# Attention, expert MLPs and a dense MLP on one core: units in turned order, two preparations a unit, last weights' halves moved

## The chip, the core and the metric

One core of a Trainium2 chip runs the whole program. The metric is the device time in microseconds (us) of one execution; of before there are three timed runs. The engines are named as in the profile: PE (TensorE; PEld is its weight load), DVE (VectorE), ACT (ScalarE), POOL (GpSimd), SP (SyncE, which here only issues DMAs).

## What is computed

Three stages, each fed by the one before; everything is float32 outside.

```python
# 1. attention: q, k, v are [4, 8, 576, 64]; heads 0-3 "plain", heads 4-7 "dilated"
scores = q @ k.T / 8
mask_plain = (rel >= 0) & (rel < 32)                       # rel = query - key
mask_dil = (rel >= 0) & (rel < 128) & (rel % 4 == 0)
attn = softmax(where(mask, scores, -1e9)) ; x = attn @ v   # -> [2304, 512] tokens
# 2. mixture of experts, 8 experts, top 1
xn, en = x / |x|, expert_emb / |expert_emb|
logits = xn @ en.T / 0.1 ; e = argmax ; gate = softmax(logits)[e]
y = gate * (relu(x @ w1[e]) @ w2[e])                       # w1 [8,512,1024], w2 [8,1024,512]
# 3. dense MLP with a per-column leak
h = y @ w_in ; g = max(h, 0) + alpha * min(h, 0) ; out = g @ w_out   # w_in [512,2048]
```

## The kernel before

**Attention** is cut into 44 units (n = 0 to 43, eleven for each of 4 batches). A unit is a block of four (in places two) score tiles of one kind, plain or dilated. It passes through the engines as a pipeline over units: in the body of unit n stand `stage_qk(n)` (mask and scores on PE, row maximum `nm` on DVE, `exp` on ACT), `stage_t(n-1)` (the exponentials are transposed on PE, L437, and brought to SBUF as `pts`), `stage_av(n-2)` (times V on PE into `o`, L458; then DVE takes the row sums, `rs`, their reciprocal and the product `xs`, L463 to L476) and, some units later, `stage_x` (`xs` transposed into `psx`, L513, and copied to `xp`/`xd`) and the router's logits. The PSUM tile `o` has one buffer, so the next AV starts only when DVE has read `o` into `xs`. Between these stand the **preparations**: the next batch's q and k are transposed, four per head pair, the plain ones in 64-column tiles (L362), the dilated ones in 128-column tiles (L365). A table `PLAN` says how many preparations each unit takes: three in most units of the first batch, then two, then one at a batch's end. The products on 64-column tiles (plain preparations and AV) are called narrow here, those on 128 columns (scores, transposes) wide. Each engine executes its instructions in the order in which the code emits them, and an instruction that waits holds all that stands behind it on its engine.

**Routing.** When a group of tokens is through, POOL scatters their numbers into the table `tab_d` (`to_table`, L552, one indirect DMA per 128 tokens), then reads indices back (`x_index`, `ix`), gathers the first slot's tokens (`x_gather`, `xg`) and builds one-hot rows (`hot`, L571 and L573), from which PE makes the ranks (`hot_rows`, `lgf`, L582). These steps hang on the units of the last batch by the list `last`; POOL also splits two of the first weight pieces (L723, L727).

**Expert MLPs.** Nine slots s = 0 to 8 of fixed widths (`WIDTHS`: 192, 256, 408, 360, 328, 312, 296, 272, 256 tokens) run in a row; each has eight steps f. In a step PE makes `hps` (layer 1, `l1`, L810), ACT and DVE split the result into a high and a low part (`hh` L814, `hl` L815), and PE makes `yps` (layer 2, `l2`, L1030) two steps later. Products are in three terms of split operands. A stream of weights is loaded ahead by SP (`w_load`, at most AHEAD = 4 items ahead, five staging tiles `stg`) and split by ACT (`whi`, L725) and DVE or POOL (`wlo`, L727, one instruction of 128x1024). Into the same stream are put the halves of the dense MLP's weights (`z_load`, `z_split`): 32 halves; the split of one is six DVE instructions (L1084 to L1091, tiles `za`, `zb`) and a copy on ACT. Before, a slot takes one half (s = 1), two at f = 0 and 2 (s = 2 to 7), or five at f = 0, 2, 3, 5, 7 (s = 8): 18 halves; the other 14 are split in the first chunk of the dense MLP. `feed(8*s + f)` emits what is due at a step. At f = 1 `y_store` writes the slot before to `y_d`; at f = 0 of slot 8 `y_load(0)` brings the dense MLP's first chunk back, and `y_split(0, f-4)` at f = 4 to 7, behind `feed`, splits it (L1106 on ACT, L1107 on DVE). `overflow` (slot 1) fills the little tile `widths` on POOL (L982) and subtracts it on DVE (L983).

**Dense MLP.** Five chunks of up to 512 tokens, sixteen steps each: `mps` (m1, L1116), the leak on ACT and DVE, `ops` (m2, L1142).

## Time and profile before

| what | us |
|---|---|
| timed runs: median (lowest to highest of 3) | 889.96 (883.88 to 895.82) |
| the profiled execution, its own time | 888.99 |
| span of its trace | 887.2 |
| PE busy in it | 836.1 (94%) |
| PE busy by stage: attention 0 to 187.4 of the span | 167.2 |
| expert MLPs, 187.4 to 467.2 | 263.6 |
| dense MLP, 467.2 to 887.2 | 405.3 |

PE is busy nearly throughout; its clock is granted at full speed (1.0 in the rows, 2.4 GHz) or at half (0.5, 1.2 GHz), and busy time in a stretch at half counts twice. So the time is to be read in two things: where PE stands still, and where it runs at half clock. DVE (52%), ACT (42%) and POOL (23%) have room on the average, but each is in order.

### The profile page before, as it was taken

How to read it: one execution, taken by the hardware profiler on the slowest of the kernel's cores; microseconds unless marked ns; L12 is line 12 of the kernel's file. 1: busy time of each engine (PE TensorE's matmuls, PEld its weight loads, DVE VectorE, ACT ScalarE, POOL GpSimd, SP SyncE). 2: the span in 40 equal slices, each digit the busy share in tenths (PEclk: the TensorE clock that was granted, in tenths of full speed). 3: DMA queues.
4: the chain of work that ended last, by engine and by line, in shares of the span. 5: the costliest groups of instructions: out<-in, count | busy, mean ns of one | idle time of the engine just before them, and what ended most of it. 6: DMA issues, size and time to landing. Idle time of an engine off the chain costs nothing.

```text
span 887.2 us, 15233 instructions
## 1 busy us (share of the span) xinstructions
PE 836.1 (94%) x5887; PEld 731.7 (82%) x5887; DVE 459.3 (52%) x959; ACT 375.7 (42%) x823; POOL 200.1 (23%) x211
## 2 busy tenths in 40 slices
PE   7999999599899999989888999999999999999994
PEld 5888887489899999989877888788888888888893
DVE  3556665356566576665678888622332233223330
ACT  3546665253545545534533443533333333333431
POOL 7100012743364457554410000000010001000100
PEclk8859999689999999989898999999999999999998
DMA  9974933746676998978973560100010001000000
GB/s 179 168 161 88 184 73 63 112 112 139 207 188 144 269 163 179 281 185 134 281 222 95 72 170 1 59 37 1 1 60 36 1 1 42 30 1 1 25 24 26
DMA packets 102093, 93.39 MB, mean 105 GB/s; under 512 B 38770, under 2 KB 83076, under 8 KB 102016
## 3 DMA queue, kind: packets, MB, share of 16 engines
q1 hardware_dynamic: 97472, 81.82, 42.2%
q0 software_dynamic: 4544, 10.54, 3.5%
q8 instruction: 48, 0.79, 0.4%
q14 instruction: 29, 0.24, 0.1%
HBM read 77.08 MB, written 15.27 MB: 104 GB/s over the span
## 4 chain that ended last, share of the span: by engine, by line
PE 70%; DMA 10%; DVE 9%; ACT 5%; issue 3%; POOL 2%; SPq 1%; POOLq 0%; ACTq 0%; DVEq 0%
PE mps L1116 21%; PE ops L1142 21%; PE hps L810 8%; PE yps L1030 7%; DMA stg<-in_moe_w_out_dram 3%; DMA stg<-in_moe_w_in_dram 3%; PE s L419 2%; PE o L458 2%; DMA kld<-in_k_dram 2%; DMA stg<-in_moe_w_dram 2%; ACT pe L426 1%; PE pt L437 1%; PE s L405 1%; PE psq L362 1%; PE psx L513 1%
## 5 line engine op out<-in xcount | busy, mean ns | idle before, releaser
L1128 DVE SCALAR_TENSOR_TENSOR g<-z,nalpha,g 128x512 f32<-128x512 f32 (+1 forms) x80 | 55.6, 695 | 169.7 <-ACT g L1127 169.6
L1116 PE MATMUL mps<-yh,zhi 128*128 128x512 f32 (+1 forms) x320 | 119.1, 372 | 1.8 <-ACT yh L1106 1.8
L1116 PE MATMUL mps<-yl,zhi 128*128 128x512 f32 (+1 forms) x320 | 118.9, 372 | 1.1 <-DVE yl L1107 1.1
L1116 PE MATMUL mps<-yh,zlo 128*128 128x512 f32 (+1 forms) x320 | 118.9, 372 | 0.0
L1154 POOL DMA_INDIRECT out_dram<-osb,cid x18 | 18.4, 1020 | 406.1 <-ACT osb L1153 371.4
L1126 ACT ACTIVATE z<-mps 128x512 f32<-128x512 f32 (+1 forms) x80 | 44.3, 554 | 150.1 <-PE mps L1116 150.1
L1142 PE MATMUL ops<-zhi,gl 128*128 128x512 f32 x256 | 100.9, 394 | 0.2 <-DVE gl L1130 0.2
L1142 PE MATMUL ops<-zhi,gh 128*128 128x512 f32 x256 | 100.8, 394 | 0.0
L1142 PE MATMUL ops<-zlo,gh 128*128 128x512 f32 x256 | 100.4, 392 | 0.0
L727 POOL TENSOR_TENSOR wlo<-stg,whi 128x1024 fp32r<-128x1024 f32 x30 | 75.4, 2513 | 95.0 <-ACT whi L725 94.7
L1030 PE MATMUL yps<-hh,whi 128*128 128x256 f32 (+7 forms) x288 | 91.2, 317 | 3.9 <-ACT hh L814 2.8
L1030 PE MATMUL yps<-hl,whi 128*128 128x256 f32 (+7 forms) x288 | 89.1, 309 | 4.0 <-DVE hl L815 3.9
L1030 PE MATMUL yps<-hh,wlo 128*128 128x256 f32 (+7 forms) x288 | 88.6, 308 | 0.0
L810 PE MATMUL hps<-xl,whi 128*128 128x256 f32 (+7 forms) x288 | 88.1, 308 | 0.3 <-DVE xl L776 0.3
L810 PE MATMUL hps<-xh,whi 128*128 128x256 f32 (+7 forms) x288 | 88.2, 308 | 0.0
L810 PE MATMUL hps<-xh,wlo 128*128 128x256 f32 (+7 forms) x288 | 88.1, 308 | 0.0
L426 ACT ACTIVATE pe<-s,nm 96x80 f32<-96x80 f32 (+1 forms) x168 | 42.0, 328 | 77.2 <-DVE nm L421 56.8
L1116 PEld LDWEIGHTS mps<-yh,zhi 128*128 128x128 f32 x320 | 60.6, 189 | 13.6 <-ACT yh L1106 2.3
L1116 PEld LDWEIGHTS mps<-yl,zhi 128*128 128x128 f32 x320 | 60.5, 189 | 13.7 <-DVE yl L1107 2.3
L725 ACT CAST whi<-stg 128x1024 fp32r<-128x1024 f32 x62 | 64.7, 1044 | 15.4 <-DMA stg<-in_moe_w_dram 14.9
L1116 PEld LDWEIGHTS mps<-yh,zlo 128*128 128x128 f32 x320 | 60.5, 189 | 10.8
L1129 ACT CAST gh<-g 128x512 fp32r<-128x512 f32 x64 | 39.7, 621 | 65.0 <-DVE g L1128 65.0
(228 smaller groups left out, 1696.0 us busy)
## 6 DMA issues: line engine op xcount, KB each, us to landing
stg<-in_moe_w_dram SPq DMA_DIRECT2D x64, 512.0 KB, 9.8
stg<-in_moe_w_in_dram SPq DMA_DIRECT2D x16, 512.0 KB, 9.0
stg<-in_moe_w_out_dram SPq DMA_DIRECT2D x16, 512.0 KB, 6.7
yl<-y_d SPq DMA_DIRECT2D x4, 1024.0 KB, 5.9
kld<-in_k_dram SPq DMA_DIRECT2D x8, 384.0 KB, 7.0
qld<-in_q_dram SPq DMA_DIRECT2D x8, 384.0 KB, 7.1
x_d<-xs SPq DMA_DIRECT2D x32, 96.0 KB, 3.5
vdl<-in_v_dram SPq DMA_DIRECT2D x16, 160.0 KB, 4.2
```

Source lines behind the costliest of these rows:

```text
L419: nc.tensor.matmul(s[0:nq, i, c0:nk], lhsT=lhsT, rhs=rhs, start=False, stop=(i == m - 1))
L426: nc.scalar.activation(out=pe[0:nq, i, :], in_=s[0:nq, i, :], func=AF.Exp, bias=nm[0:nq, i:i + 1])
L725: nc.scalar.copy(hi, s)
L727: eng.tensor_tensor(out=lo, in0=s, in1=hi.bitcast(F32), op=ALU.subtract)
L810: nc.tensor.matmul(ps, lhsT=parts[j][0][:, kk, :], rhs=parts[j][1][:, kk, 0:wd], start=((kk, j) == steps[0]), stop=((kk, j) == steps[-1]))
L1030: nc.tensor.matmul(ypt[s_, d], lhsT=a[:, 128 * d:128 * (d + 1)], rhs=x, start=(f == 0 and j == 0), stop=(f == NF - 1 and j == 2))
L1116: nc.tensor.matmul(ps, lhsT=a[:, kk, :], rhs=x, start=(kk == 0 and j == 0), stop=(kk == KD - 1 and j == 2))
L1126: nc.scalar.activation(out=z, in_=ps, func=AF.Relu, scale=-1.0)
L1128: vec.scalar_tensor_tensor(out=g, in0=z, scalar=nalpha[:, f:f + 1], in1=g, op0=ALU.mult, op1=ALU.add)
L1129: nc.scalar.copy(gh, g)
L1142: nc.tensor.matmul(opt[c, t], lhsT=a[:, 128 * t:128 * (t + 1)], rhs=x, start=(f == 0 and j == 0), stop=(f == NF2 - 1 and j == 2))
L1154: nc.gpsimd.indirect_dma_start(out=out[:, :], out_offset=bass.IndirectOffsetOnAxis(ap=cid[:, 4 * c + t, 0:1], axis=0), in_=o, in_offset=None)
```

## The change

1. `PLAN` becomes `PREPS = 2`: two preparations in every unit.
2. In odd units from n = 3 on the narrow work (plain preparations, AV) is emitted ahead of the wide work (scores, transposes, dilated preparations); in even units the order stays.
3. The first batch's q and k of the dilated heads are loaded ahead of its plain v.
4. In the last batch `to_table` is no longer called after every unit but once, behind two of the three one-hot builds; `hot_rows` of groups 1 and 2 and of group 0 move by a unit or more, the third into slot 0's hooks.
5. `widths` is filled in the setup.
6. POOL's `wlo` is cut in four instructions of 256 columns (for s > 0); DVE's is not.
7. `z_split` works in place, in the staging tile, with one temporary tile in place of two; the staging counter starts at 1.
8. The weights' halves per slot become 1, 3, 3, 2, 2, 1, 1, 4 for s = 1 to 8, at the steps in `ZAT`: 17 in place of 18, so 15 are left for the dense MLP.
9. `y_split(0, .)` comes at f = 3 to 6 of slot 8, ahead of `feed`; `y_load(0)` and slot 0's `y_store` are issued on ACT's queue in place of SP's.

```diff
-    PLAN = ((2, 3, 3, 3, 3, 3, 3, 3, 3, 3, 3), (2, 2, 2, 2, 2, 2, 2, 1, 1, 1, 1))
+    PREPS = 2
...
+    load_qk(0, 0, 1)
     load_vpl(0)
-    load_qk(0, 0, 1)
...
+        for i in range(NS):
+            nc.gpsimd.memset(widths[:, i:i + 1], float(WIDTHS[i]))
...
-    ns_ = [0]
+    ns_ = [1]
...
-        eng.tensor_tensor(out=lo, in0=s, in1=hi.bitcast(F32), op=ALU.subtract)
+        n = 256 if eng is nc.gpsimd and i else 1024
+        for c in range(0, 1024, n):
+            eng.tensor_tensor(out=lo[:, c:c + n], in0=s[:, c:c + n], in1=hi[:, c:c + n].bitcast(F32), op=ALU.subtract)
...
-    for i, f in ((0, regs_a), (0, lambda: x_index(0)), (1, open_early), (1, flush), (1, lambda: x_gather(0)), (1, to_table),
-                 (2, hg(0)), (2, wl(0)), (3, hg(1)), (3, wl(1)), (4, hg(2)), (4, wl(2)), (5, wl(3)), (5, hr(0)), (5, sp(0)),
-                 (6, wl(4)), (6, sp(1)), (7, hr(1)), (8, hr(2)), (9, lambda: x_turn(0, 0)), (10, lambda: x_turn(0, 1))):
+    for i, f in ((0, regs_a), (0, lambda: x_index(0)), (1, open_early), (1, flush), (1, lambda: x_gather(0)), (1, hg(0)),
+                 (2, hg(1)), (2, to_table), (2, wl(0)), (3, hg(2)), (3, wl(1)), (4, wl(2)), (5, wl(3)), (5, sp(0)),
+                 (6, wl(4)), (6, sp(1)), (6, hr(0)), (8, hr(1)), (9, lambda: x_turn(0, 0)), (10, lambda: x_turn(0, 1))):
...
+            def wide():
+                stage_qk(n, u)
...
+            def narrow():
+                some(plains[1])
+                some(plains[0], 1)
+                if n >= 2:
+                    stage_av(n - 2)
+                some(plains[0])
...
+            for f in (narrow, wide) if n % 2 and n > 2 else (wide, narrow):
+                f()
...
-            to_table()
+            if b < 3:
+                to_table()
...
-            nc.sync.dma_start(
+            (nc.sync if s_ else nc.scalar).dma_start(
...
-        a = tmp_p.tile([128, 512], I32, tag="t", name="za")
...
+        vec.tensor_scalar(out=b, in0=whi, scalar1=3, scalar2=0x3FFFFFF8, op0=ALU.logical_shift_left, op1=ALU.bitwise_and)
+        vec.scalar_tensor_tensor(out=whi, in0=whi, scalar=-0x40000000, in1=b, op0=ALU.bitwise_and, op1=ALU.bitwise_or)
+        vec.tensor_scalar(out=b, in0=whi, scalar1=-0x800000, scalar2=None, op0=ALU.bitwise_and)
...
+    ZAT = ((), (0,), (0, 2, 4), (0, 2, 4), (0, 3), (0, 3), (2,), (2,), (2, 3, 5, 7))
...
-            if f in ((0, 2, 3, 5, 7) if s_ == NS - 1 else (0, 2) if s_ > 1 else (0,)):
+            if f in ZAT[s_]:
...
-        2: [do(hot, 3, vec)],
+        2: [do(hot, 3, vec), do(hot_rows, 2)],
...
-                y_load(0)
+                y_load(0, nc.scalar)
+            if s_ == NS - 1 and 2 < f < 7:
+                y_split(0, f - 3)
             feed(8 * s_ + f)
-            if s_ == NS - 1 and f > 3:
-                y_split(0, f - 4)
```

On PE, before, in the third batch's end (a unit's scores `s`, transposes `pt` and `psx`, then its AV into `o`; here the AV of a dilated block, and that of a plain one a unit later):

```order
L419 MATMUL s<-kpl_156,qpl_138 128x96 x2
L437 MATMUL pt<-idf,pe 96x128 x4
L513 MATMUL psx<-idf,xs 128x112 x2
L365 MATMUL psq<-idf,qld 128x48 x4
L458 MATMUL o<-vdl_154,pts 64x65
L458 MATMUL o<-vdl_154,pts 48x65
...
L406 LDWEIGHTS e_dl
L406 MATMUL s<-mask_0_227,e_dl 96x320
L419 MATMUL s<-kdl_157,qdl_139 96x80 x4
L437 MATMUL pt<-idf,pe 96x128 x2
L513 MATMUL psx<-idf,xs 128x112 x2
L458 MATMUL o<-vpl_152,pts 64x65 x8
```

The same place of the changed kernel:

```order
L422 MATMUL s<-kpl_157,qpl_139 128x96 x2
L440 MATMUL pt<-idf,pe 96x128 x4
L516 MATMUL psx<-idf,xs 128x112 x2
L461 MATMUL o<-vdl_155,pts 64x65
L461 MATMUL o<-vdl_155,pts 48x65
...
L461 MATMUL o<-vpl_153,pts 64x65 x8
L409 LDWEIGHTS e_dl
L409 MATMUL s<-mask_0_228,e_dl 96x320
L422 MATMUL s<-kdl_158,qdl_140 96x80 x4
L440 MATMUL pt<-idf,pe 96x128 x2
L516 MATMUL psx<-idf,xs 128x112 x2
```

The two AVs stand back to back, with no scores or transposes between them, and the two wide parts that follow stand together as well.

On POOL, before, at the start of the last batch (`tab_d<-row` is a scatter, `xg<-x_d` a gather, `hot` a one-hot build of one group):

```order
L552 DMA tab_d<-row,idxi 18432x1 x12
L757 TENSOR_TENSOR ix_309<-ix_309 128x2 x2
L761 DMA xg<-x_d,ix_309 128x512
L761 DMA xg<-x_d,ix_309 64x512
L571 TENSOR_SCALAR rel<-idxf,val_a 128x4
L573 TENSOR_SCALAR hot<-count,rel 128x256 x4
```

The same place of the changed kernel, down to POOL's first weight split:

```order
L555 DMA tab_d<-row,idxi 18432x1 x9
L763 TENSOR_TENSOR ix_310<-ix_310 128x2 x2
L767 DMA xg<-x_d,ix_310 128x512
L767 DMA xg<-x_d,ix_310 64x512
L574 TENSOR_SCALAR rel<-idxf,val_a 128x4
L576 TENSOR_SCALAR hot<-count,rel 128x256 x4
L574 TENSOR_SCALAR rel<-idxf,val_a 128x4
L576 TENSOR_SCALAR hot<-count,rel 128x256 x4
L555 DMA tab_d<-row,idxi 18432x1 x3
L574 TENSOR_SCALAR rel<-idxf,val_a 128x4
L576 TENSOR_SCALAR hot<-count,rel 128x256 x4
L726 CAST whi<-stg 128x1024
```

The second three of the scatters now stand behind two one-hot builds.

On DVE, before, at the start of slot 6 (`hl` is the low part of layer 1's result, `za` and `zb` the split of a weights' half, `ys` the copy of the slot before, `wlo` a split of a piece):

```order
L815 SCALAR_TENSOR_TENSOR hl<-hps,hh 128x296
L1084 TENSOR_SCALAR za<-stg 128x512
L1085 SCALAR_TENSOR_TENSOR za<-stg,za 128x512
L1086 TENSOR_SCALAR zb<-za 128x512
L1088 SCALAR_TENSOR_TENSOR zb<-stg,zb 128x512
L1090 TENSOR_TENSOR za<-za,zhi 128x512
L1091 TENSOR_TENSOR zlo<-za,zb 128x512
L815 SCALAR_TENSOR_TENSOR hl<-hps,hh 128x296
L1038 COPY ys<-yps 128x312 x2
L727 TENSOR_TENSOR wlo<-stg,whi 128x1024
L815 SCALAR_TENSOR_TENSOR hl<-hps,hh 128x296
L1084 TENSOR_SCALAR za<-stg 128x512
```

The same place of the changed kernel:

```order
L821 SCALAR_TENSOR_TENSOR hl<-hps,hh 128x296 x2
L1049 COPY ys<-yps 128x312 x2
L733 TENSOR_TENSOR wlo<-stg,whi 128x1024
L821 SCALAR_TENSOR_TENSOR hl<-hps,hh 128x296
L1096 TENSOR_SCALAR zb<-stg 128x512
L1097 SCALAR_TENSOR_TENSOR stg<-stg,zb 128x512
L1098 TENSOR_SCALAR zb<-stg 128x512
L1099 SCALAR_TENSOR_TENSOR zb<-stg,zb 128x512
L1101 TENSOR_TENSOR stg<-stg,zhi 128x512
L1102 TENSOR_TENSOR zlo<-stg,zb 128x512
```

One of the two half splits that stood here is gone; the one left stays behind the third `hl`.

## Rows read from the trace of the kernel before

**Rows 1.** By stretch: length, busy time of PE, PEld, DVE, ACT, POOL, granted clock.

```profile
48.20:68.70 20.50, 20.50 (x194) 18.20 (x193) 10.13 (x39) 8.04 (x26) 0.00 (x0) 0.50 0.73 152
68.70:158.70 90.00, 87.69 (x1308) 75.30 (x1306) 58.43 (x206) 54.49 (x175) 9.36 (x10) 1.00 0.50 97
158.70:169.60 10.90, 1.45 (x26) 1.05 (x26) 1.31 (x5) 1.28 (x5) 8.79 (x13) 0.60 0.72 41
...
371.60:406.30 34.70, 30.69 (x206) 30.08 (x205) 21.12 (x29) 16.41 (x30) 19.55 (x14) 0.90 0.77 204
406.30:438.90 32.60, 29.11 (x203) 28.26 (x201) 19.92 (x28) 14.34 (x27) 15.61 (x12) 0.90 0.90 197
438.90:467.20 28.30, 24.00 (x195) 23.19 (x194) 21.53 (x35) 11.05 (x21) 6.19 (x3) 1.00 0.84 207
467.20:477.10 9.90, 6.93 (x27) 5.02 (x26) 6.87 (x13) 2.66 (x5) 0.00 (x0) 0.71 0.32 105
477.10:887.20 410.10, 398.38 (x1825) 328.57 (x1824) 171.80 (x291) 146.27 (x281) 18.36 (x18) 0.99 0.13 34
```

**Rows 2.** Waits of PE: line waited for, us in total, times, longest.

```profile
PE lgf L582 <- POOL hot L573: 9.4, 4, 7.3
...
PE psx L513 <- ACT qdl L118: 1.7, 1, 1.7
```

**Rows 3.** Timeline of PE, first 30 us: start, duration, instruction, idle before and releaser.

```profile
15.01 0.90 PE L365 MATMUL psq<-idf,qld 96*128 96x96 f32 x4 [1.06 <-DMA qld<-in_q_dram]
...
21.20 1.09 PE L362 MATMUL psq<-idf,kld 48*64 48x48 f32 x16 [1.19 <-DMA kld<-in_k_dram]
```

**Rows 4.** Timeline of PE in a unit of the last batch at full clock.

```profile
153.35 0.49 PE L437 MATMUL pt<-idf,pe 96*80 96x96 f32 x4
153.68 0.38 PE L513 MATMUL psx<-idf,xs 128*128 128x128 f32 x2
154.00 0.69 PE L458 MATMUL o<-vpl,pts 96*64 96x65 f32 x16
```

**Rows 5.** Timeline of DVE behind that AV.

```profile
155.14 0.42 DVE L476 TENSOR_TENSOR xs<-o,rs 128x256 f32<-128x256 f32 x1
```

**Rows 6.** Timeline of POOL in the last batch.

```profile
160.78 0.96 POOL L552 DMA_INDIRECT tab_d<-row,idxi  x1 [0.46 <-issue]
...
181.81 2.36 POOL L727 TENSOR_TENSOR wlo<-stg,whi 128x1024 fp32r<-128x1024 f32 x1
```

**Rows 7.** Timeline of DVE in slot 1.

```profile
235.59 0.17 DVE L983 TENSOR_TENSOR ex<-seg,widths 128x9 f32<-128x9 f32 x1 [3.60 <-POOL widths L982]
```

**Rows 8.** Timeline of PE in slot 1.

```profile
237.36 0.66 PE L773 MATMUL xps<-idf,xg 128*128 128x128 f32 x4 [3.24 <-DVE hl L815]
```

**Rows 9.** Timeline of DVE in slot 6.

```profile
375.47 2.56 DVE L1086 TENSOR_SCALAR zb<-za 128x512 int32<-128x512 int32 x1
...
388.76 1.78 DVE L1084 TENSOR_SCALAR za<-stg 128x512 int32<-128x512 int32 x1 [6.01 <-DMA stg<-in_moe_w_out_dram]
...
391.30 0.43 DVE L1086 TENSOR_SCALAR zb<-za 128x512 int32<-128x512 int32 x1
```

**Rows 10.** Timeline of POOL in slot 6.

```profile
374.90 2.84 POOL L727 TENSOR_TENSOR wlo<-stg,whi 128x1024 fp32r<-128x1024 f32 x1 [0.45 <-ACT whi L725]
```

**Rows 11.** Timeline of SP, the issues of transfers, in slots 6 and 8.

```profile
375.33 0.35 SPq L1068 DMA_DIRECT2D stg<-in_moe_w_out_dram  x1
...
439.74 0.49 SPq L1097 DMA_DIRECT2D yl<-y_d  x1
...
453.82 0.40 SPq L1050 DMA_DIRECT2D y_d<-ys  x1
```

**Rows 12.** Timeline of PE in slot 6.

```profile
394.21 0.69 PE L773 MATMUL xps<-idf,xg 128*128 128x128 f32 x2 [4.01 <-DVE hl L815]
```

**Rows 13.** Timeline of DVE, a half's split in the dense MLP, first and last of six.

```profile
548.90 0.42 DVE L1084 TENSOR_SCALAR za<-stg 128x512 int32<-128x512 int32 x1
...
551.87 0.69 DVE L1091 TENSOR_TENSOR zlo<-za,zb 128x512 fp32r<-128x512 f32 x1
```

More of the change, by code (lines that the diff above doesn't have):

```diff
@@ L97 @@
     enT = const.tile([128, KD, 32], F32, name="enT")
+    widths = const.tile([128, NS], F32, name="widths")
     load = {"v": 0.0, "a": 0.0}
@@ L854 @@
                 route_after(n - 3)
-            np_ = PLAN[min(b, 1)][i]
+            np_ = PREPS
             pq, rq = prepq[:np_], routeq.pop(0) if routeq else []
@@ L871, in some @@
                 del fs[:cnt]
-            stage_qk(n, u)
-            some(lts)
-            some(dils[0], 1)
-            if n >= 1:
-                stage_t(n - 1)
-            some(dils[0])
-            some(turns)
-            some(dils[1])
-            some(plains[1])
-            some(plains[0], 1)
-            if n >= 2:
-                stage_av(n - 2)
-            some(plains[0])
+            def wide():
+                stage_qk(n, u)
+                some(lts)
+                some(dils[0], 1)
+                if n >= 1:
+                    stage_t(n - 1)
+                some(dils[0])
+                some(turns)
+                some(dils[1])
+            def narrow():
[6 more added lines that the diff above has]
+                f()
             some(lgs)
@@ L979, in overflow @@
         tot = so.tile([P, 1], F32, name="tot")
-        widths = so.tile([P, NS], F32, name="widths")
-        for i in range(NS):
-            nc.gpsimd.memset(widths[:, i:i + 1], float(WIDTHS[i]))
         vec.tensor_tensor(out=ex, in0=seg[:, :, 0], in1=widths, op=ALU.subtract)
@@ L1081, in z_split, with y_load @@
         hi, lo = (a[:, 512 * s_:512 * (s_ + 1)] for a in zpc[p])
-        a = tmp_p.tile([128, 512], I32, tag="t", name="za")
         b = tmp_p.tile([128, 512], I32, tag="t", name="zb")
-        vec.tensor_scalar(out=a, in0=whi, scalar1=3, scalar2=0x3FFFFFF8, op0=ALU.logical_shift_left, op1=ALU.bitwise_and)
-        vec.scalar_tensor_tensor(out=a, in0=whi, scalar=-0x40000000, in1=a, op0=ALU.bitwise_and, op1=ALU.bitwise_or)
-        vec.tensor_scalar(out=b, in0=a, scalar1=-0x800000, scalar2=None, op0=ALU.bitwise_and)
-        fa, fb = a.bitcast(F32), b.bitcast(F32)
-        vec.scalar_tensor_tensor(out=fb, in0=wlo.bitcast(U32), scalar=2.0 ** -52, in1=fb, op0=ALU.mult, op1=ALU.mult)
-        nc.scalar.copy(hi, fa)
-        vec.tensor_tensor(out=fa, in0=fa, in1=hi.bitcast(F32), op=ALU.subtract)
-        vec.tensor_tensor(out=lo, in0=fa, in1=fb, op=ALU.add)
-    def y_load(c):
+        bf, wf = b.bitcast(F32), whi.bitcast(F32)
+        vec.tensor_scalar(out=b, in0=whi, scalar1=3, scalar2=0x3FFFFFF8, op0=ALU.logical_shift_left, op1=ALU.bitwise_and)
+        vec.scalar_tensor_tensor(out=whi, in0=whi, scalar=-0x40000000, in1=b, op0=ALU.bitwise_and, op1=ALU.bitwise_or)
+        vec.tensor_scalar(out=b, in0=whi, scalar1=-0x800000, scalar2=None, op0=ALU.bitwise_and)
+        vec.scalar_tensor_tensor(out=bf, in0=wlo.bitcast(U32), scalar=2.0 ** -52, in1=bf, op0=ALU.mult, op1=ALU.mult)
+        nc.scalar.copy(hi, wf)
+        vec.tensor_tensor(out=wf, in0=wf, in1=hi.bitcast(F32), op=ALU.subtract)
+        vec.tensor_tensor(out=lo, in0=wf, in1=bf, op=ALU.add)
+    def y_load(c, eng=nc.sync):
         m = min(CH, NTOK - CH * c)
         yt[c] = (xy_l if (NS + c) % 2 else xy_e).tile([128, KD, 512], F32R, tag="xl", name="yl")
-        nc.sync.dma_start(out=yt[c].bitcast(F32)[:, :, 0:m],
+        eng.dma_start(out=yt[c].bitcast(F32)[:, :, 0:m],
                           in_=y_d[:, CH * c:CH * c + m].rearrange("(k p) t -> p k t", p=128))
```

## The prediction

> **What bounds the kernel now.** First the table of busy times: PE is busy in 836.1 of 887.2 us, so the time is PE's work, the places where PE stands, and the stretches in which its clock is granted at half. The second view is busy time by stretch [rows 1]: length minus PE's busy time is where PE stands, and (1 − granted clock) times length is what half clock (1.2 GHz) costs there, if PE has work all the time. The third is PE's list of waits [rows 2]; the last is the timelines of the engines that PE waits for. They show five places that the change touches.
>
> 1. Attention, 48.2 to 68.7: PE has no idle time but runs at 0.50, which costs up to 10.3 us [rows 1]. Ahead of it PE had waited 1.7 us for the dilated queries `qdl` from ACT [rows 2].
> 2. End of attention, 158.7 to 169.6: PE is busy 1.45 of 10.9 us [rows 1]; 9.4 us are waits of the ranks (`lgf`) for POOL's one-hot rows [rows 2].
> 3. Slot 1: DVE waits 3.60 us for POOL to fill `widths` [rows 7]. Behind that stands `hl`, and PE stands 3.24 us for it [rows 8].
> 4. Slots 6, 7 and 8: PE stands 34.70−30.69 = 4.0, 32.60−29.11 = 3.5 and 28.30−24.00 = 4.3 us; half clock costs 0.10×34.70 = 3.5 and 0.10×32.60 = 3.3 us more in 6 and 7 [rows 1]. In slot 6 the cause is that a weights' half was issued at 375.33 [rows 11] and DVE waited for it, with `hl` behind, from 382.75 to 388.76, 6.01 us [rows 9]; PE then waited 4.01 us for `hl` [rows 12].
> 5. Start of the dense MLP, 467.2 to 477.1: 9.90−6.93 = 3.0 us standing and 0.29×9.90 = 2.9 us of half clock [rows 1], while the chunk's `y_split` is late.
>
> From 477 on PE is busy 398.4 of 410.1 us at 0.99 [rows 1]: nothing to win there.
>
> **The change, part by part**, against the profiled execution's 889.0 us (the median of the three runs is 890.0, 1.0 higher).
>
> *Start.* The dilated q and k are loaded ahead of v. PE waits 1.06 and 1.19 us for them now [rows 3]; I take both as gone: −2.3. If v is late in their place, 0; nothing else there is ahead of them.
>
> *Turned order, up to unit 27.* In every odd unit the AV now follows the AV of the unit before, 21 pairs. `o` has one buffer, so the second AV waits until DVE has written `xs`: AV ends at 154.00+0.69 = 154.69 [rows 4], `xs` at 155.14+0.42 = 155.56 [rows 5], 0.87 us, with the way to PE about 0.95. In seven pairs two plain preparations stand between (one takes 1.09 at half clock [rows 3], so some 0.55 at full, two about 1.1): covered, I put 0.1 each. In five the router's logits stand between, about half as much: 0.47 each. In nine there is nothing: 0.95 each. Up to unit 27 there are 7, 3 and 3 of these: 0.7+1.4+2.9 = +5.0. Behind the second AV are queued the wide parts of two units, but DVE and ACT get the same work in pairs, so I add 1.5 for transposes that come before their exponentials are ready (bounds 0 to 4; two wide parts give 2 us to a chain that needs most of that). In return PE changes between narrow and wide tiles half as often. What a change costs: the four transposes of 96 columns begin 0.33 us before what follows, 0.00086 a column; the two of 128 columns ahead of AV should then take 0.22 and take 0.32 [rows 4]. So 0.10, the same for the way back, 0.2 for each of 12 pairs: −2.4 (bounds 0 and −4). The idle time now in 68.7 to 158.7 is 2.3 us [rows 1], most of it the uneven preparations: −2.3. Together +1.8, rounded to +2.
>
> *The half-clock stretch.* With two preparations a unit the 1.7 us wait for `qdl` has no reason to be where it is; but another wait may come. At worst the 10.3 us stay (or come elsewhere), at best about 9 are won (part of that work is not clock-bound). I take half: −4.5.
>
> *End of attention, units 28 on.* Nine scatters, gathers, two builds, then three scatters: in front of the first build three scatters fewer stand, but the gathers' indices wait for a reading of the table anyway (the last of the twelve began at 160.78 with a gap of 0.46 [rows 6]), so gathers and builds come about 1 us earlier only, while all that follows comes three scatters (3×1.3) less that 1 us later: POOL's last weight split, which ended at 181.81+2.36 = 184.2 [rows 6], ends near 187. Layer 1 of slot 0 began at 187.4 and needs those splits, so at most 3 us can be won there, however much of the 9.4 us of waiting goes; pairs without cover (six here, 5.7 us) fill what was idle. I take −2.2 (bounds −3 and +3, where +3 is POOL's delay handed on in full).
>
> *`widths`.* Filled in the setup, the wait of DVE has no object; nine small fills lie in POOL's idle time in the setup. −3.2, since PE's 3.24 us hang on that wait alone; it costs nothing elsewhere.
>
> *Halves moved, pieces of POOL's split, split in place.* Slots 6 and 7 lose the half at f = 0 and keep the one at f = 2. With one item less in the stream its load is emitted about a step (3.5 us) earlier, and one transfer of 512 KB less stands with it; against 6.01 us of waiting, of which the first 2 did not reach PE (6.01−4.01), that leaves no or little stall. DVE is also spared a split whose third instruction took 2.56 us [rows 9] while POOL's `wlo` ran 2.84 [rows 10], in place of 0.43 [rows 9]; cut in four, POOL can hold it up by a quarter, 0.7. Of 4.0+3.5 and 3.5+3.3 I take −6 and −6 (bounds 0 and −14.3). Slot 8 has four halves in place of five, −2.5 of 4.3, since `y_split` now comes a step earlier, ahead of them. Start of the dense MLP: `y_split` done a step earlier, −5 of 3.0+2.9 and the 0.6 of half clock behind 477.1. Together −19.5 (bounds −25 and 0). Slots 2 and 3 get a third half: DVE there is paid from idle time, and I put nothing. The price if it is not covered is in the second rival.
>
> Slot 8's transfer of `yl` was issued by SP at 439.74, and the store behind it, which waits for its end, at 453.82 [rows 11]: 14 us under way while the transfers' engines are at 0.84 [rows 1]. Now ACT issues it, and slot 0's store, each for about the 0.5 us that SP was held (ACT has idle time in both places, so nothing). If its own queue carried it past the halves, it would land before the first `y_split` (f = 3, some 10.5 us into the slot), and slot 8 would win all 4.3; if it shares the engines as before, the split waits some 3 us and holds ACT's `hh` behind it. I take the second, hence 2.5 and not 4.3. The Trainium skill says so too (Trainium Kernel Development and Optimization, Key Constraints: the queues of SP, ACT and POOL run on the same 16 DMA engines, and another queue only saves issue time); by it the move is worth no more than SP's issue, and the sum stays as it is.
>
> *Dense MLP.* One half more is split in chunk 0, six instructions from 548.90 to 551.87+0.69, 3.7 us [rows 13]; DVE has about 3 us left in that step: +0.7 (bounds 0 and 3.7).
>
> **Sum:** −2.3 +2 −4.5 −2.2 −3.2 −19.5 +0.7 = −29.0, 860.0 for the profiled execution, 861 for the median.
>
> **The rivals.**
>
> *The stall moves (A).* DVE's room in slots 2 and 3 is on the average; a third half at f = 4 may wait for its transfer as the second did in slot 6, or `y_split` at f = 3 waits for `yl` and hands it on through ACT. Then half of the 19.5 is lost (9.7) and up to two new stalls come, each some 2 to 4 us with up to 3.5 of half clock. For it speaks the 0.77 to 0.90 of the transfers' engines in these slots, against it that each slot that stalled now has less to load. 869 to 878.
>
> *The clock falls in attention (B), the other side.* The 0.95 us in which PE stands between paired AVs comes every second unit, in the stretch of 90 us that ran at 1.00 [rows 1]. A wait of 1.7 us was followed by 20.5 us at 0.50 [rows 1, 2]. Each such stretch costs 10.3: with two, 861+20.6 = 882, with three 892, no gain at all. It decides from 28 us on, that is 56 of the 90 us at half clock. Against it: a pair's wait is about half of that one, and busy work stands before and after. 878 to 900.
>
> *All stalls gone (C).* Slots 6 to 8 and the dense MLP's start give all of 25, and attention stays at full clock (−9): 5.5+4.5 = 10 us better, 845 to 853.
>
> **How the numbers follow.** Forecast, 853 to 869: 0.50. C: 0.15. A: 0.20. B: 0.12. Anything worse: 0.03. The range 846 to 885 takes in most of C, all of A and about half of B, and leaves out about 0.12. A measurement of this kernel tells about 2% from no change, so faster means below 872: the forecast, C and some 0.3 of A, less a little for unknown bounds, 0.70. Slower means above 908: 0.04. The rest, 0.26.
>
> **What would show it.** Start: no wait for `qld` and `kld` in PE's list. Turned order: `o` waiting for `xs`, about 1 us each and some 14 times; granted clock 1.0 from 30 to 158. End of attention: POOL's last weight split near 187 less what was won before it. Slot 1: no wait of `ex`. Slots 6 and 7: DVE's wait for a half under 2 us, granted clock 1.00, PE standing under 1 us. Dense MLP's start: no waits for `yh` and `yl`. It is wrong if attention as a whole (0 to layer 1 of slot 0) is not shorter than now, or if slots 2 and 3 show new waits for `hl`.

## The result, and the profile after

The changed kernel is slower by about 1%: median 898.65 us against 887.9 us, ratio 1.0114 (95% interval 1.0086 to 1.0142). Forecast were 861 us and a gain. Ratios leave out the executions that took over 1.5% longer than the fastest of their kernel. The experiments ran in three groups, each with the kernel before beside it (medians 878.2, 880.0 and 878.0 us); there the changed kernel's ratio was 1.0215 (1.0157 to 1.0272). So ratios to the kernel before of the same group are compared below, and inside one profile the stages.

Cut at the same instructions of PE, the two profiled spans (887.2 and 895.6 us) differ like this. (In units 3 and 27 of the changed kernel the AV stands ahead of the scores, so the AV of one unit changes sides at each of these two cuts.) "Step" is one of the sixteen steps of a chunk in the dense MLP; the forecast is the sum's own term.

| stretch | before | after | forecast | measured |
|---|---|---|---|---|
| start to the scores of unit 3 | 31.1 | 27.3 | −2.3 | −3.8 |
| units 3 to 27 (order +2, clock −4.5) | 91.7 | 102.0 | −2.5 | +10.3 |
| unit 27 to layer 1 of slot 0 | 64.6 | 64.0 | −2.2 | −0.6 |
| slot 0 | 29.2 | 33.1 | 0 | +3.9 |
| slot 1 (`widths`) | 26.1 | 22.5 | −3.2 | −3.6 |
| slots 2 and 3 | 68.4 | 74.1 | 0 | +5.7 |
| slots 4 and 5 | 60.5 | 60.7 | 0 | +0.2 |
| slots 6 and 7 | 67.3 | 56.6 | −12 | −10.7 |
| slot 8 and the dense MLP's first four steps | 53.9 | 53.4 | −7.5 | −0.5 |
| the dense MLP's steps 5 to 16 | 66.3 | 72.7 | +0.7 | +6.4 |
| the rest | 328.2 | 329.2 | 0 | +1.0 |
| sum | 887.2 | 895.6 | −29.0 | +8.3 |

What was forecast as a gain came in the start, slot 1 and slots 6 and 7, at nearly its size (−18.1 for −17.5). Four places failed: units 3 to 27 with the turned order and the clock, slots 2 and 3, slot 8 with the dense MLP's start, and the one half more in the dense MLP. Busy time by stretch of the kernel before (length, then busy time of PE, PEld, DVE, ACT, POOL, granted clock, share of the transfers' engines, GB/s), for the two stretches that have no row in [rows 1]:

```profile
31.10:122.80 91.70, 88.96 (x1261) 78.46 (x1259) 57.37 (x189) 56.14 (x169) 0.00 (x0) 0.89 0.67 134
...
492.80:559.10 66.30, 66.30 (x290) 54.11 (x289) 56.82 (x102) 26.58 (x49) 0.00 (x0) 1.00 0.41 87
```

The same view of the changed kernel, units 3 to 27, the rest of attention, slots 0, 3, 6, 7, 8, and the dense MLP's steps 5 to 16:

```profile
27.30:129.30 102.00, 90.96 (x1304) 82.12 (x1303) 57.17 (x191) 58.74 (x173) 0.00 (x0) 0.88 0.67 138
129.30:193.30 64.00, 49.30 (x640) 41.35 (x635) 31.61 (x124) 26.46 (x98) 32.53 (x35) 0.97 0.43 92
...
193.30:226.40 33.10, 30.14 (x265) 28.48 (x263) 19.14 (x67) 13.01 (x28) 9.35 (x11) 0.90 0.60 97
...
285.50:323.10 37.60, 34.81 (x206) 34.47 (x206) 25.89 (x35) 17.19 (x31) 21.52 (x24) 0.95 0.75 194
383.80:413.00 29.20, 27.91 (x206) 27.51 (x206) 14.63 (x23) 15.45 (x29) 17.68 (x23) 1.00 0.76 204
413.00:440.40 27.40, 25.71 (x202) 25.30 (x201) 13.72 (x22) 13.47 (x26) 18.56 (x23) 1.00 0.93 205
440.40:473.80 33.40, 25.65 (x195) 25.02 (x194) 20.75 (x35) 11.45 (x22) 10.01 (x12) 0.85 0.71 173
...
493.80:566.50 72.70, 69.93 (x290) 56.09 (x289) 62.56 (x114) 29.84 (x54) 0.00 (x0) 0.95 0.43 88
```

Slots 6 and 7 now run at full clock with 1.3 and 1.7 us of standing, where it was 4.0 and 3.5 at 0.90 [rows 1]. Units 3 to 27 have 11.0 us of standing in place of 2.7, at the same clock (0.88 for 0.89), and the first four steps of the dense MLP, in which PE before waited twice (1.82 us for `yh`, 1.15 for `yl`), have no such wait: it has moved into slot 8, where PE stands 7.7 us at a clock of 0.85. The waits of PE in the changed kernel (us in total, times, longest) name what is new:

```profile
PE o L461 <- DVE xs L479: 12.9, 12, 1.6
PE yps L1041 <- ACT hh L820: 6.5, 1, 6.5
...
PE psl L529 <- ACT xd L119: 4.5, 4, 1.4
```

The 9.4 us of waits for the one-hot rows, which headed this list in [rows 2], are gone from it. They were not won: from unit 27 on the waits of `o` for `xs` (5.3 us, 4 times) and of the logits for `xd` (4.5) stand in their place.

A pair of AVs at units 28 and 29, on PE (start, duration, instruction, idle before and releaser):

```profile
139.40 0.68 PE L461 MATMUL o<-vdl,pts 80*64 80x65 f32 x16
141.28 0.69 PE L461 MATMUL o<-vpl,pts 96*64 96x65 f32 x16 [1.20 <-DVE xs L479]
...
143.25 0.51 PE L525 MATMUL psl<-xp,enT 128*32 128x192 f32 x2
145.06 0.28 PE L529 MATMUL psl<-xd,enT 128*32 128x96 f32 x2 [1.30 <-ACT xd L119]
```

And DVE's work between the two:

```profile
140.14 0.33 DVE L466 TENSOR_SCALAR rs<-o 64x4 f32<-64x4 f32 x2
140.50 0.18 DVE L469 RECIPROCAL rs<-rs 112x4 f32<-112x4 f32 x1
140.71 0.42 DVE L479 TENSOR_TENSOR xs<-o,rs 112x256 f32<-112x256 f32 x1
```

This uncovered pair costs 1.20 us, not 0.95: behind a dilated block `rs` is made in two pieces. (The twelve waits of `o` for `xs` lie between 0.37 and 1.62 us.) And 2 us later PE stops a second time, since in a turned unit the logits come right behind the transposes whose copies (`xd`) they read; in the old order an AV stood between.

### The profile page after: what moved, and what is told of

It is laid out like the page before. It is cut to its first block, busy times and chain, and to the rows that moved or that the text cites. A ratio compares the mean times of both kernels' runs of the same rounds, so it can differ in the third digit from the quotient of the medians.

```text
span 895.6 us, 15336 instructions
## 1 busy us (share of the span) xinstructions
PE 832.5 (93%) x5887; PEld 733.3 (82%) x5887; DVE 454.6 (51%) x956; ACT 379.8 (42%) x826; POOL 219.2 (24%) x295
## 5 line engine op out<-in xcount | busy, mean ns | idle before, releaser
L733 POOL TENSOR_TENSOR wlo<-stg,whi 128x256 fp32r<-128x256 f32 (+1 forms) x114 | 96.4, 874 | 72.7 <-ACT whi L728 69.7
```

The source lines that it names most:

```text
L733: eng.tensor_tensor(out=lo[:, c:c + n], in0=s[:, c:c + n], in1=hi[:, c:c + n].bitcast(F32), op=ALU.subtract)
```

## Experiments

Each edit is against the changed kernel, or, where it says so, against the kernel before. The lengths of stages come from each run's profile. The "mean clock" is the mean granted clock over all timed runs of a kernel in one group; (1 − mean clock) times the time is what half clock costs it. PE "stands" for the length of a stretch less its busy time.

### The turned order

The changed kernel itself, beside the others:

> The changed kernel itself, unaltered, beside the others of this call on one chip. Expected by every theory: ratio 1.008 to 1.015 to the kernel before; layer 1 of slot 0 begins 5 to 12 us later than in the kernel before, slot 8 takes 31 to 34 us, PE waits 4 us or more for hh there.

The old order in every unit:

```diff
-            for f in (narrow, wide) if n % 2 and n > 2 else (wide, narrow):
-                f()
+            wide()
+            narrow()
```

> The changed kernel with the old order in every unit (wide work, then narrow work); everything else of the change stays, two preparations a unit too. Theory 1 (the paired AVs cost the time in attention): in the changed kernel layer 1 of slot 0 begins at 193.3 us, 10.2 of them lost between units 3 and 27; without the pairs PE's waits of o for xs (12.9 us, 12 times) go and layer 1 begins at 183 to 187, the whole 7 to 10 us faster than the changed kernel, about 888. Rival (the even spread of preparations, or the new place of the scatters and one-hot builds, costs it): layer 1 still begins within 2 us of 193, and the whole stays at about 897.

Only the preparations turned, AV behind the wide work again:

```diff
+            turned = n % 2 and n > 2
...
-                if n >= 2:
+                if not turned and n >= 2:
                     stage_av(n - 2)
...
+            if turned:
+                stage_av(n - 2)
```

> The changed kernel, but in the turned units only the plain preparations are ahead of the wide work; AV is behind it again, so that no two AVs are neighbours. Theory 1a (what costs is the second AV's wait for the one buffer of o): PE's waits of o for xs vanish as in the kernel with the old order, layer 1 of slot 0 at 183 to 187. Theory 1b (what costs is that logits follow right behind the transposes of xs, and that two wide parts follow one another): the waits of psl for xd (4.5 us) and of pt for its copies stay, layer 1 at 189 to 193.

And the turned order alone, put into the kernel before (the `wide`/`narrow` lines of the change and nothing else):

> The kernel before with the turned order in odd units alone, everything else as before. Theory 1 (the pairs cost by themselves, whatever the preparations are): PE waits of o for xs 9 to 13 us in all, about half of it ahead of unit 27, layer 1 of slot 0 begins 6 to 10 us later than in the kernel before, ratio 1.005 to 1.012. Rival (the turned order costs only together with two preparations a unit): ratio 0.997 to 1.003.

| kernel | ratio to before (95%) | mean clock |
|---|---|---|
| changed | 1.0215 (1.0157 to 1.0272) | 0.949 |
| changed, old order | 0.9883 (0.9794 to 0.9971) | 0.971 |
| changed, AV back | 0.9863 (0.9759 to 0.9967) | 0.960 |
| before, turned order alone | 1.0366 (1.0311 to 1.0421) | 0.938 |
| before | 1 | 0.96 |

Attention up to layer 1 of slot 0, in the view of busy time by stretch: changed; before with the turned order; changed with the old order; changed with AV back; and the kernel before with `widths` moved (an experiment below; its attention is that of the kernel before). The last two rows are the two profiles of the result, before and changed:

```profile
0.00:212.60 212.60, 176.83 (x2182) 152.37 (x2182) 100.62 (x339) 95.74 (x294) 53.32 (x104) 0.85 0.61 115
...
0.00:220.00 220.00, 187.37 (x2189) 161.35 (x2190) 102.45 (x339) 95.75 (x294) 52.91 (x95) 0.78 0.57 112
...
0.00:170.30 170.30, 154.08 (x2182) 130.38 (x2182) 102.92 (x347) 93.10 (x290) 53.28 (x104) 0.97 0.74 143
...
0.00:185.90 185.90, 170.28 (x2182) 145.32 (x2182) 101.75 (x342) 95.13 (x294) 53.28 (x104) 0.87 0.66 131
...
0.00:183.40 183.40, 168.78 (x2188) 143.06 (x2189) 101.53 (x345) 94.05 (x291) 53.12 (x104) 0.88 0.69 133
...
0.00:187.40 187.40, 167.19 (x2190) 140.19 (x2190) 101.45 (x345) 93.81 (x291) 52.82 (x95) 0.87 0.69 130
...
0.00:193.30 193.30, 164.07 (x2181) 142.36 (x2181) 100.27 (x339) 95.89 (x294) 53.30 (x104) 0.90 0.64 127
```

PE stands 35.8 and 32.6 us with the turned AVs and 14.6 to 16.2 without them, whichever kernel they are in (29.2 and 20.2 in the profiles of the result, where 9.4 of the 20.2 are the waits for the one-hot rows). So of the turned order it is the AVs that cost (theory 1a): with AV back, the waits of `o` for `xs` are gone, and of those of the logits for `xd` 0.6 us are left. The rival that the even preparations cost it falls with the old order alone, and the rival that the order costs only together with them falls with the turned order in the kernel before, where it cost most: 3.7%, three times what was expected. (Two more expectations were missed: the changed kernel lost 2.2% where 0.8 to 1.5% were expected, and with the old order layer 1 began at 170.3 us, ahead of the expected 183 to 187, in an attention that ran at a clock of 0.97.) PE's waits in attention in the kernel before with the turned order:

```profile
PE o L458 <- DVE xs L476: 10.9, 10, 1.6
PE psl L526 <- ACT xd L118: 3.3, 3, 1.4
PE pt L437 <- ACT pts L118: 3.2, 6, 1.3
```

Of the 32 us that this kernel lost (0.0366 of 880), standing is 32.6−14.6 = 18.0. The rest, some 14 us, goes with the clock: 0.78 over its attention against 0.88, and 187.4 us of busy time against 168.8 for all but the same number of products. Its four runs have clocks of 0.935 to 0.943, below all thirteen of the kernel before (0.950 to 0.967). By the means of all runs half clock costs (1−0.938)×912 = 57 us there, (1−0.949)×899 = 46 in the changed kernel, 35.8 in the kernel before (0.9592 of 879.0) and 25 to 35 without the pairs. In one profile the clock scatters a good deal (0.97 and 0.87 for two kernels whose PE stands equally long), so only the means are compared.

So the wait on the one buffer is shown, and for the kernel before with the turned order a fall of the granted clock too. For the changed kernel the second is less sure: its four clocks (0.939 to 0.953) overlap with those of the kernel before, and in the two profiles of the result attention ran at 0.90 against 0.87 and lost by standing alone (29.2 against 20.2 us, while busy time fell from 167.2 to 164.1).

### Slot 8 and the dense MLP's start

The early split of the first chunk undone, in the changed kernel and then together with the old order:

```diff
-            if s_ == NS - 1 and 2 < f < 7:
-                y_split(0, f - 3)
             feed(8 * s_ + f)
+            if s_ == NS - 1 and f > 3:
+                y_split(0, f - 4)
```

> The changed kernel with the split of the dense MLP's first chunk back at f = 4 to 7 of slot 8, behind the feed. Theory 2 (the split at f = 3 holds ACT: it waits 10.7 us until the store of slot 7 has landed at 462.4, since its tile is the one that slot 7's result is stored from, and hh stands behind it): slot 8 falls from 33.4 us to 29 to 30, PE's wait of 6.45 us for hh to under 3, the whole 3 to 4 us faster than the changed kernel, about 894 to 895. Rival (the late halves of the weights hold slot 8 anyway): slot 8 stays at 32 to 34 us, and the whole at 897 to 899.

> The changed kernel with the old order in every unit and with the split of the first chunk back at f = 4 to 7 behind the feed: the two suspects undone together. Theories 1 and 2: attention as in the kernel with the old order alone (that one: ratio 0.988), slot 8 at 24 us in place of 32 to 33, a part of which comes back as waits at the start of the dense MLP; 3 to 5 us less than the old order alone, ratio 0.982 to 0.985. Rival (slot 8's wait only moves into the dense MLP): ratio 0.987 to 0.990.

What was read in the changed kernel, on ACT, and what SP waited for in slot 8:

```profile
451.36 0.38 ACT L820 ACTIVATE hh<-hps 128x256 fp32r<-128x256 f32 x1
462.47 0.62 ACT L1117 CAST yh<-yl 128x512 fp32r<-128x512 f32 x1 [10.73 <-DMA y_d<-ys]
```

```profile
SPq L1061 <- DMA yl<-y_d: 9.2, 1, 9.2
```

The high part `yh` is put into the tile from which slot 7's result is stored to `y_d` (`ys` and `yh` are both the tag "xh" of one pool), and that store waits until the reading of `yl` from `y_d` is over. So the split waits for the store's landing, not only for `yl`, and with the early split ACT stands before `hh`. The move of `y_load` to ACT's queue did not help: `yl` was issued at 442.20 and the store behind it at 456.46, 14.3 us later, where it was 14.1 before [rows 11]; its own queue did not carry it past the halves. With the split undone in the changed kernel, slot 8 takes 23.8 us, less than the 29 to 30 expected, but the ratio is 1.0187 (1.0058 to 1.0315), with an attention of 214 us in the profile. Together with the old order the ratio is 0.9889 (0.9833 to 0.9945), against 0.9883 with the old order alone. Slot 8 and the dense MLP, early split and then late split, both with the old order:

```profile
403.20:435.80 32.60, 26.19 (x194) 25.59 (x193) 19.25 (x36) 11.36 (x21) 8.42 (x11) 0.90 0.69 170
435.80:856.50 420.70, 405.79 (x1850) 333.52 (x1849) 179.33 (x304) 149.55 (x285) 18.80 (x18) 0.99 0.14 37
```

```profile
411.10:435.80 24.70, 23.69 (x194) 23.25 (x193) 15.01 (x27) 8.83 (x16) 7.47 (x11) 1.00 0.89 227
435.80:862.90 427.10, 408.56 (x1850) 334.79 (x1848) 184.14 (x313) 152.51 (x291) 19.30 (x18) 0.98 0.14 37
```

Slot 8 falls to 24.7 us as theory 2 said, but the dense MLP gives 6.4 of the 7.9 us back: the ratio is the rival's. (Together the two stages are 1.5 us shorter in this pair of profiles and 4.9 us in the pair with the turned order; the ratios show neither.) The place of the split mostly decides where the one wait is paid: from slot 8's start to the fifth step of the dense MLP it is 51.7 to 53.9 us in every kernel so far, before the change too. The next runs show a part of what makes that chain so long.

### The stores of 4 bytes

In nearly every slot, in all profiles of kernels with these stores, the transfers nearly stop for some 9 us, beginning about 3 us after the sums of squares (`ssq`) are stored. The suspicion was that store, since its numbers lie singly, 4 bytes each and side by side. In the kernel before:

```diff
-    ssq_d = dram.tile([YW, 1], F32, name="ssq_d")
+    ssq_d = dram.tile([YW, 16], F32, name="ssq_d")
...
-    ssq = const.tile([128, NS, 4], F32, name="ssq")
+    ssq = const.tile([128, 4, 4, 16], F32, name="ssq")
...
-            "(c p) o -> p (c o)", p=128), in_=ssq[:, s_, 0:n])
+            "(c p) o -> p c o", p=128), in_=ssq[:, s_ % 4, 0:n])
```

> The kernel before, but each slot's sums of squares are stored as rows of 64 bytes, not as single neighbouring numbers of 4 bytes (the other 15 numbers of a row are unused); nothing else. Theory 4 (the stores of 4 bytes, issued at 243, 276, 310, 343, 373, 406 and 439 us, are what brings all transfers nearly to a stand 3 us later: 25 GB/s from 376 to 386 against 301 ahead of it): the rate stays above 150 GB/s there, DVE's waits for halves of the weights (31 us between 200 and 480) fall under 12, PE's waits for hl and hh in slots 6 to 8 mostly go, 6 to 12 us faster than before, ratio 0.987 to 0.993. Rival (the gathers and the other transfers of that stretch do it): rate and waits as before, ratio 0.998 to 1.002.

Measured: 0.9911 (0.9867 to 0.9955). Busy time by stretch around slot 6's store, first in the kernel before (issued at 373.1; the last number of a row is GB/s, the one ahead of it the share of the transfers' engines), then with rows of 64 bytes (issued at 371.4):

```profile
363.00:373.00 10.00, 10.00 (x74) 9.76 (x73) 4.98 (x8) 6.79 (x15) 5.99 (x4) 1.00 1.05 301
...
376.00:386.00 10.00, 10.00 (x73) 9.82 (x72) 6.68 (x9) 3.62 (x7) 6.14 (x6) 1.00 0.36 25
```

```profile
361.00:371.00 10.00, 10.00 (x73) 9.57 (x72) 6.64 (x9) 6.52 (x15) 5.43 (x4) 1.00 0.83 233
...
374.00:384.00 10.00, 10.00 (x73) 9.90 (x72) 9.79 (x15) 5.15 (x9) 7.77 (x7) 1.00 0.80 193
```

25 GB/s at a share of 0.36 becomes 193 at 0.80. DVE's waits for halves of the weights between 200 and 480 were 17.9+13.3 = 31.2 us in the profile of the kernel before, and 10.3+6.5 = 16.8 in that of the kernel with `widths` moved, whose stores are the same; now they are this:

```profile
DVE za L1087 <- DMA stg<-in_moe_w_in_dram: 1.5, 1, 1.5
```

The transfers were not slow because there were many of them, as the prediction had it, but because one of 1.5 KB stood in the way. The rival (gathers) falls. The rate still drops for shorter times (33 GB/s from 282.6 to 286.0, behind the store issued at 276.6); whether loads were outstanding then is not told apart. The Trainium skill (DMA: Bandwidth & Descriptors, Specifications) says that below 512 bytes a transfer does a read-modify-write and misses line rate. That goes with the 4 bytes being slow, but 64 bytes are below that limit too and the stop of some 9 us is gone, in the same number of pieces; what differs (neighbours sharing a piece of memory) is not told apart here.

### Where the halves stand

The new places alone, in the kernel before:

```diff
+    ZAT = ((), (0,), (0, 2, 4), (0, 2, 4), (0, 3), (0, 3), (2,), (2,), (2, 3, 5, 7))
...
-            if f in ((0, 2, 3, 5, 7) if s_ == NS - 1 else (0, 2) if s_ > 1 else (0,)):
+            if f in ZAT[s_]:
```

> The kernel before with the new places of the weights' halves alone (1, 3, 3, 2, 2, 1, 1, 4 in slots 1 to 8). By the comparison of the two profiled kernels: slots 6 and 7 fall to 27.7 to 29 and 25.3 to 27 us, slots 2 and 3 grow by 1 to 4 us each, and the dense MLP behind its first three steps takes 4 to 6 us more, for the half that is left to it. Theory: these cancel, ratio 0.995 to 1.003. Rival (the new places win what was forecast for them, 12 us in slots 6 and 7 and nothing lost elsewhere): ratio 0.985 to 0.990.

Measured: 0.9952 (0.9910 to 0.9993). Slots 2, 3, 6 and 7:

```profile
236.70:271.80 35.10, 35.10 (x207) 34.96 (x206) 28.33 (x35) 17.49 (x31) 17.64 (x12) 1.00 0.75 202
271.80:306.40 34.60, 33.53 (x205) 33.17 (x204) 26.56 (x35) 16.92 (x31) 17.85 (x12) 1.00 0.80 210
366.20:393.90 27.70, 27.70 (x206) 27.51 (x205) 16.64 (x23) 15.55 (x29) 15.52 (x13) 1.00 0.80 215
393.90:419.50 25.60, 25.40 (x202) 25.18 (x201) 15.97 (x22) 13.44 (x26) 14.99 (x11) 1.00 0.89 218
```

Slots 6 and 7 are free of stops, slot 3 pays 1.1 us, slot 2 nothing, and the dense MLP's steps 5 to 16 take 71.0 us in place of 66.3. The gain is half a per cent, not 12 us: in other profiles slots 6 and 7 as they were before lose less to begin with (28.8 and 29.8 us in the run with `widths` moved, 28.4 and 30.4 in that with the turned order alone, 34.7 and 32.6 in [rows 1]).

One half more ahead of the dense MLP, in slot 6, with the old order:

```diff
-    ZAT = ((), (0,), (0, 2, 4), (0, 2, 4), (0, 3), (0, 3), (2,), (2,), (2, 3, 5, 7))
+    ZAT = ((), (0,), (0, 2, 4), (0, 2, 4), (0, 3), (0, 3), (2, 5), (2,), (2, 3, 5, 7))
```

> The changed kernel with the old order in every unit and one half of the weights more in slot 6 (at f = 5): 18 halves ahead of the dense MLP, as before the change, in place of 17. Theory 5 (the fifteenth half in the dense MLP's first chunk comes a step too late: PE waits 1.7 us for its high part and 1.1 us for its low part, and the clock falls for 6.8 us behind): both waits go, the dense MLP from its first step on takes 420 less 5, about 415 to 416 us, ratio to before 0.982 to 0.984 (the old order alone: 0.988). Rival (the half's split now holds slot 6): slot 6 grows from 27.7 to 30 us or more, ratio 0.986 to 0.990.

The two waits in the changed kernel that it aimed at, and the dense MLP's steps 5 to 16 with one half more ahead:

```profile
552.48 0.50 PE L1127 MATMUL mps<-yh,zhi 128*128 128x512 f32 x1 [1.68 <-ACT zhi L1100]
...
554.30 0.80 PE L1127 MATMUL mps<-yh,zlo 128*128 128x512 f32 x1 [1.09 <-DVE zlo L1102]
```

```profile
481.20:547.90 66.70, 66.70 (x290) 54.19 (x290) 57.43 (x103) 27.85 (x51) 0.00 (x0) 1.00 0.40 87
```

66.7 us at full clock in place of 72.7 at 0.95 (and 66.7 in both kernels of the next group): theory 5 held. But the ratio was 0.9892 (0.9820 to 0.9963), no better than the old order's 0.9883. In the profile slot 6 took 32.6 us in place of 27.7, as the rival had it; that execution took 879.8 us where the kernel's median is 868.5, so whether slot 6 always pays is left open.

### Together

The old order, 18 halves and rows of 64 bytes; then the same with the late split of the first chunk:

> The same as the kernel with the old order and 18 halves, and the sums of squares stored as rows of 64 bytes. Theory 4 (the stores of 4 bytes make the halves and the reading of y late): slot 8 falls from 32 to 33 us to 26 to 28, since the chain from the reading of y over slot 7's store to the split of the first chunk shortens by 5 us or more; slot 3's waits go; ratio 0.970 to 0.977. Rival (slot 8's chain is set by something else): slot 8 stays above 31 us, ratio as without the wide rows.

> The same again, with the split of the first chunk back at f = 4 to 7 behind the feed. If the place of the split only moves one and the same wait between slot 8 and the dense MLP's start (as the old order with and without the later split showed: slot 8 24.7 in place of 32.6 us, the dense MLP 427.1 in place of 420.7), slot 8 and the dense MLP together differ by less than 2 us from the kernel with the early split. If the early split is worth something once the transfers are quick, the late one is 3 to 5 us slower.

0.9742 (0.9664 to 0.9821) and 0.9810 (0.9735 to 0.9885). Slot 8 in the first and in the second:

```profile
413.30:439.90 26.60, 25.06 (x194) 24.66 (x194) 20.09 (x33) 11.33 (x21) 7.97 (x10) 0.94 0.62 201
```

```profile
408.70:431.80 23.10, 23.10 (x195) 23.10 (x194) 18.26 (x31) 10.69 (x20) 8.03 (x10) 1.00 0.72 231
```

From slot 8's start to the fifth step of the dense MLP they take 46.6 and 47.8 us, where the same kernel with stores of 4 bytes takes 53.0: the stop of the transfers held some 6 us of that chain. (In the kernel before the wide rows alone make 50.1 of 53.9.) Slot 8 and the dense MLP together are 444.5 and 445.0 us, so the place of the split is worth nothing measurable here either. Slot 6 takes 28.3 us with its two halves, slot 3 33.2. The first of the two has the lowest median of this study, 856.1 us against 878.0 for the kernel before (the second, at 857.9, is not told apart from it); both are faster than both given kernels.

### `widths` alone

The fills moved to the setup, in the kernel before:

> The kernel before with the fills of widths moved to the setup, nothing else. Theory 3 (PE's 3.24 us in slot 1 hang on that wait alone): slot 1 falls from 26.1 to about 22.8 us, the whole 3.2 us faster than before, ratio 0.996. Rival (the next wait of DVE takes its place): slot 1 stays above 25 us, ratio 0.999 to 1.001.

```profile
210.10:232.60 22.50, 22.15 (x184) 21.79 (x185) 14.70 (x41) 12.88 (x30) 8.81 (x8) 1.00 0.80 258
```

Slot 1 takes 22.5 us in place of 26.1, as expected (22.5 to 22.6 in every profile with the fills moved, 26.1 to 29.7 in every one without); the ratio, 0.9971 (0.9927 to 1.0015), agrees with 3.2 us but does not exclude none.

## Why the prediction was wrong

*Start*, −2.3: −3.8 to unit 3; the wait for `kld` is gone, one of 0.7 us for `qld` stays. No run has this part alone.

*Turned order*, +2, and *half-clock stretch*, −4.5: wrong, and the largest error. Up to unit 27 −2.5 was forecast and +10.3 measured, and the profile splits the difference. The step "AV, `xs`, AV" was the right mechanism, and its price was somewhat low: eight waits of 0.37 to 1.48 us, 7.5 us in all, where the working had 5.0. What failed was the gains that were to pay for it. The rest of PE's standing is 11.0−7.5 = 3.5 us against 2.7 before, so the −2.3 for even preparations did not come. Busy time is 91.0 us against 89.0 (1304 products against 1261), at a clock of 0.88 against 0.89, so neither the −4.5 of the clock nor the −2.4 for fewer changes of tile is to be seen (no run has the price of such a change alone). The step on the clock was that the stretch at half clock goes if the wait of 1.7 us for `qdl` goes. That wait is gone, and a stretch of 20.5 us at half clock is still there, only earlier:

```profile
24.50:45.00 20.50, 19.30 (x168) 17.64 (x170) 9.25 (x34) 8.32 (x28) 2.47 (x15) 0.50 0.96 204
```

With AV back, and no wait for `qdl` either, it lies from 51.3 to 71.8; with the old order there is none from 18.1 to 161.5. What it hangs on stays open.

Behind unit 27 the clause that the pairs "fill what was idle" was wrong too: the wait for the one-hot rows was gone, and standing from 129.3 to 193.3 was 64.0−49.3 = 14.7 us, against 12.4 before. The logits' stop behind a pair (four, 1.1 us on the average) was not in the sum at all: the working asked who stands between two AVs, not from whose cover the AV was taken away.

The rival B, which had 0.12, named the time (878 to 900), but by luck: it wanted two or three stretches at half clock, 10.3 us each, where attention had run at full clock, and in the profile of the result half clock cost attention (1−0.90)×193.3 = 19 us, against (1−0.87)×187.4 = 24 before. What B described is seen in the turned order put into the kernel before. One sign that the prediction had set for being wrong came true here, attention longer than before (193.3 us against 187.4), and the other in slots 2 and 3 (PE waits 4.1 us for `hl`).

*End of attention*, −2.2: −0.6. POOL's last weight split ended at 190.0, where the working had near 187. But that split was not the bound that the working took it for: PE's first product of layer 1 follows the product ahead of it without a gap in both profiles, 3.3 us behind that split here and 12.9 us behind it in the second profile of the changed kernel, and with one half more in slot 6 it came 1.0 us ahead of the split's end. Layer 1 begins when PE's own queue reaches it, with the waits above in it.

*Slot 0*, 0: +3.9 in the profile of the result, where a piece of weights landed late (ACT waited 4.45 us for it, PE then 1.9 and 0.8) and the clock was 0.90. In the other profiles with the new slot 0 it takes 26.8 to 34.9 us, in those with the old one 26.6 to 29.2; what of it is the change's is not told apart.

*`widths`*, −3.2: right, −3.6, and alone.

*Slots 6 and 7*, −12: −10.7, and by the reason given, a load issued a step earlier. In slot 6 the half that was issued 3.7 us into the slot, behind the store of `ssq` (landing in 13.4 us), is now issued at its start, ahead of that store (issued at 384.32), lands in 3.7 us, and DVE splits it without a wait:

```profile
383.80 0.35 SPq L1079 DMA_DIRECT2D stg<-in_moe_w_out_dram  x1
...
393.12 0.42 DVE L1096 TENSOR_SCALAR zb<-stg 128x512 int32<-128x512 int32 x1
```

That the load had to be ahead of that store was not known, and the size is partly luck: the profile that the forecast was read from had 67.3 us in slots 6 and 7, two others of the same slots 58.6 and 58.8, and with the new places alone they take 53.3, some 5 us less.

*Slots 2 and 3*, 0: +5.7, and +0.6 to +4.0 in the profiles of the other kernels with these places and stores of 4 bytes. That is the rival A in its place; the cover named, DVE's idle time on the average, was not there, since the third half's load falls into the same stop (with rows of 64 bytes slot 3 takes 33.2 us with its three halves, as before with two).

*Slot 8 and the dense MLP's start*, −7.5: −0.5. The step that failed is "the split done a step earlier": a split is not earlier for being emitted earlier when its tile comes free with a store that waits for a load. The tile was to be read in the code, and that the store waits for `yl` the working itself says.

*Dense MLP*, +0.7: +6.4. The bound of 3.7 us counted DVE's work alone; two waits, 2.8 us together, came, and half clock behind them (0.95 over 72.7 us, 3.6 us), which the term had left out.

*Pieces of POOL's split, split in place*, 0: the change does what it says only in part. In slot 8, beside POOL's four pieces, DVE's six instructions took 5.5 us (from 449.17 to 454.66) against 5.8 (from 374.30 to 380.08) in the kernel before: the third no longer takes 2.56 us [rows 9] but 0.84, while its neighbours lose:

```profile
449.68 1.09 DVE L1097 SCALAR_TENSOR_TENSOR stg<-stg,zb 128x512 int32<-128x512 int32 x1
450.80 0.84 DVE L1098 TENSOR_SCALAR zb<-stg 128x512 int32<-128x512 int32 x1
451.68 1.11 DVE L1099 SCALAR_TENSOR_TENSOR zb<-stg,zb 128x512 f32<-128x512 uint32 x1
452.71 1.22 DVE L1101 TENSOR_TENSOR stg<-stg,zhi 128x512 f32<-128x512 f32 x1
```

Each of these takes 0.4 to 0.7 us where POOL has no `wlo` beside them (slot 6, from 393.12 on). The Trainium skill (SBUF — State Buffer, Who interferes with whom) has it that a DVE instruction with two inputs in SBUF contends with a POOL instruction that reads SBUF, and that `tensor_scalar` can enter a two-port mode, in which whoever issues first has the shared pair for the whole instruction. These rows agree with it: three of the four have two inputs in SBUF and one is a `tensor_scalar` (whether in that mode, no run shows). It looks like four short locks in place of one long one, with nearly the same sum, but no run took the pieces away alone.

## What to carry to other kernels

When work is reordered, list for every instruction that now has a new neighbour whose wait its old neighbour covered, on both sides of the place; a buffer that is single makes any two of its users that become adjacent pay its whole round trip. Price a new wait with the clock behind it, as the old waits were priced; but book no gain in clock for one wait that goes (the stretch at half clock stayed here), and look up a stall that is seen in one profile in a second one (slots 6 and 7 took 67.3 us in one, 58.6 in another). And when transfers are late although their engines are not busy (a share of 0.36 at 25 GB/s), look for a small scattered store ahead of them before moving loads about.
